# Attention with mask clusters: one row for the negated maximum, queries in token order, float64 words joined with two VectorE operations and one more on ScalarE

## The chip, the cores and the metric

The program runs on one core of one Trainium2 chip. The metric is the device time of one execution in microseconds (us), as the median of several runs. The core has five engines with a queue of instructions each: PE (TensorE, matmuls), DVE (VectorE), ACT (ScalarE), POOL (GpSimd) and SP (SyncE, which here issues DMAs).

## The reference, cut to what matters

Three layers follow each other: attention over 2 batches x 8 heads x 768 tokens x 64, in which a query sees only the keys of its own cluster; a dense layer 512 -> 2048 -> 512 with a Mish activation; and a layer of 8 experts with top-1 routing and a capacity.

```python
scale = 1.0 / np.sqrt(D)
q_assign = np.argmax(np.einsum('bhsd,hcd->bhsc', q_n, c_n), axis=-1)
k_assign = np.argmax(np.einsum('bhsd,hcd->bhsc', k_n, c_n), axis=-1)
mask = q_assign[:, :, :, None] == k_assign[:, :, None, :]
scores = scale * np.matmul(q, k.transpose(0, 1, 3, 2))
scores = np.where(mask, scores, -1000000000.0)
scores = scores - np.max(scores, axis=-1, keepdims=True)
attn = np.exp(scores)
attn = attn / (np.sum(attn, axis=-1, keepdims=True) + 1e-09)
...
h = x @ w_in
sp = np.where(h > 20.0, h, np.log1p(np.exp(np.minimum(h, 20.0))))
g = h * np.tanh(sp)
...
y = np.einsum('ecf,efd->ecd', np.maximum(np.einsum('ecd,edf->ecf', disp, w1), 0.0), w2)
```

The dense layer's weights arrive as float64, since a numpy scalar made them so; the kernel turns them into float32 itself.

## The kernel before

The order of every engine's instructions is the order in which the program is written (a manual schedule); nothing is moved later. Attention works on 8 pairs (one batch, two heads). `Attention.plan` (L472) gives each piece of work a step number, and `advance` (L616) runs the steps in order. A pair has 12 steps; step s scores one block of 128 keys against 384 queries of both heads (`score`, L374), runs `pv` (L405) for the step before, and computes one unit of row maxima for a pair further on (`max_unit`, L330: two matmuls on PE, one `reduce_max` on DVE, L346), 11 steps ahead. Two PSUM areas take turns for the scores and the maxima, so PE can begin the next unit of maxima only when DVE has read the last one. Where a function returns a closure, that runs at the head of the next step.

What the change touches:

- `load` (L202) reads queries, keys and values of a pair with the token number as `(p j)`: partition p holds the tokens 6p to 6p+5. The transposed columns are therefore in the order j, p and not in token order. `xparts` and `xnorm` (L454, L461) undo this where the attention's result is written: `norm3` (L464) writes the high part of x on ACT (L467) and its low part on DVE (L468) with every sixth column, 24 bytes apart.
- `max_split` (L348) runs on DVE at the end of each half pair (16 times): L353 writes the negated maximum rounded to fp32r, L354 copies it, L355 computes what the rounding left. `max_put` (L359) transposes these 12 columns on PE, copies them out of PSUM on ACT (L364), and sends them with four small DMAs into rows 96 and 97 of `QA`. `score` multiplies them with rows of ones in `KA`, which subtracts the maximum inside the matmul (98 rows).
- `Narrow` (L627) turns 32 chunks of float64 weights (128 x 512 words of 8 bytes) into float32, 28 of them inside the attention, 4 later (`rest`, L638). A chunk takes `bias` on ACT (L676: the high word times a power of two), then on DVE `up` (L680: shift left by 3), `low` (L685: the top three bits of the low word) and `sign` (L692), then a store. `plan` deals these out by `SLOTS`: 13 slots in 12 steps, three to a chunk, so that the order recurs every 36 steps.
- POOL adds up the exponentials (`add_up`, L394, L403) and applies the reciprocal sum (L442, L452).
- SP issues all loads, stores and the copies inside the chip (`spread`, L307).

```python
            for s, g in ((s0 - 1, N.bias), (s0, N.up), (s1, N.low), (s2, N.sign), (s2 + 1, N.store)):
                at(s, g, c)
```

Of the kernel before, what the change touches and what calls it, by code (L numbers as in the profile page):

```python
# [10 lines left out]
F32 = mybir.dt.float32  # L11
F32R = mybir.dt.float32r
BF16 = mybir.dt.bfloat16
I32 = mybir.dt.int32
U32 = mybir.dt.uint32
AF = mybir.ActivationFunctionType
ALU = mybir.AluOpType
AX = mybir.AxisListType
# [4 lines left out]
def f32(ap):  # L23
    return ap.bitcast(F32)
# [144 lines left out]
class Attention:  # L169
# [32 lines left out]
    def load(self, i, names):  # L202
        nc, S = self.nc, self.S
        b, hp = self.pairs[i]
        st = self.st.setdefault(i, {})
        for nm, src, bufs in (("q", self.q, 2), ("k", self.k, 1), ("v", self.v, 2)):
            if nm not in names:
                continue
            s = src[b, 2 * hp:2 * hp + 2].rearrange("h (p j) d -> p h j d", p=128)
            if nm == "v":  # L210
                t = self.p.tile([128, 2, self.NK, self.D], F32, tag=f"{nm}n", name=f"{nm}n{i}", bufs=bufs)
                nc.sync.dma_start(out=t, in_=s)
            else:
                t = self.early.tile([128, self.NK, 2, self.D], F32, tag=f"{nm}n", name=f"{nm}n{i}", bufs=bufs)
                for h in range(2):
                    nc.sync.dma_start(out=t[:, :, h, :], in_=s[:, h])
            st[nm] = t
# [129 lines left out]

    def max_split(self, i, r):  # L348
        nc, st = self.nc, self.st[i]
        m = st["m", r]  # L350
        mm = st["mm", r] = self.p.tile([128, 2, 2, 3], F32, tag="mm", name="mm")
        mr = self.p.tile([128, 2, 3], F32R, tag="mr", name="mr")
        nc.vector.tensor_scalar_mul(out=mr, in0=m, scalar1=-1.0)  # L353
        nc.vector.tensor_copy(out=mm[:, :, 0, :], in_=f32(mr))  # L354
        nc.vector.scalar_tensor_tensor(  # L355
            out=mm[:, :, 1, :], in0=m, scalar=-1.0, in1=f32(mr), op0=ALU.mult, op1=ALU.subtract
        )

    def max_put(self, i, r):  # L359
        nc, K, st = self.nc, self.K, self.st[i]  # L360
        pt = K.misc("pmt")
        nc.tensor.transpose(pt[0:12, 0:128], st["mm", r].rearrange("p h l t -> p (h l t)"), K.ident)
        mt = self.p.tile([12, 128], F32R, tag="mt", name="mt")
        nc.scalar.activation(out=mt, in_=pt[0:12, 0:128], func=AF.Copy)  # L364
        QA = self.QA[i % 3]
        for h in range(2):
            for l in range(2):
                e = nc.gpsimd if i + r + h == 0 else nc.sync
                e.dma_start(
                    out=f32(QA[96 + l:97 + l, h, 384 * r:384 * r + 384].rearrange("a (t p) -> a t p", t=3)),  # L370
                    in_=f32(mt[6 * h + 3 * l:6 * h + 3 * l + 3, :]),
                )

    def score(self, s):  # L374
        nc, K = self.nc, self.K
# [7 lines left out]
        for h in range(2):  # L383
            nc.tensor.matmul(  # L384
                ps[:, h, 0:384], lhsT=KB[:, h, ks], rhs=QB[:, h, qs], start=True, stop=False
            )
            nc.tensor.matmul(  # L387
                ps[:, h, 0:384], lhsT=KA[0:98, h, ks], rhs=QA[0:98, h, qs], start=False, stop=True
            )
        pt = self.p.tile([128, 2, 384], F32, tag="P", name="P", bufs=4)  # L390
        nc.scalar.activation(out=pt, in_=ps[:, :, 0:384], func=AF.Exp, scale=1.0 / float(self.D) ** 0.5)  # L391
# [62 lines left out]
    def xparts(self, i, r):  # L454
        b, hp = self.pairs[i]
        return (
            a[b][:, hp, :].rearrange("d (p j) -> d j p", j=6)[:, 3 * r:3 * r + 3, :]
            for a in (self.K.xh, self.K.xl)
        )

    def xnorm(self, i, r):  # L461
        return self.st[i]["x", r].rearrange("d (j p) -> d j p", j=3)

    def norm3(self, i, r):  # L464
        hi, lo = self.xparts(i, r)
        x = self.xnorm(i, r)
        self.nc.scalar.activation(out=hi, in_=x, func=AF.Copy, scale=-1.0)  # L467
        return lambda: self.nc.vector.scalar_tensor_tensor(  # L468
            out=lo, in0=x, scalar=-1.0, in1=f32(hi), op0=ALU.mult, op1=ALU.subtract
        )  # L470

    def plan(self, N):  # L472
# [50 lines left out]
        slots = [w for w in slots if w >= self.N0]  # L523
        for c in range(N.CUT):
            s0, s1, s2 = slots[3 * c:][:3]
            for s, g in ((s0 - 1, N.bias), (s0, N.up), (s1, N.low), (s2, N.sign), (s2 + 1, N.store)):
                at(s, g, c)
            if c + 3 < N.CUT:
                at(s2 + self.NL, N.load, c + 3)
# [97 lines left out]
class Narrow:  # L627
# [10 lines left out]
    def rest(self):  # L638
# [3 lines left out]
        for c in range(self.CUT, self.N):  # L642
            self.bias(c)
            yield
            self.up(c)
            yield
            self.low(c)
            yield
            self.sign(c)
            if c + 3 < self.N:  # L650
# [21 lines left out]
    def bias(self, c):  # L672
# [2 lines left out]
        r = self.res[c] = self.p.tile([128, 512], I32, tag="n32", name=f"n32_{c}", bufs=3 if c < self.CUT else 2)  # L675
        self.nc.scalar.activation(out=f32(r), in_=f32(hi), func=AF.Copy, scale=2.0 ** -112)  # L676

    def up(self, c):
        r = self.res[c]
        self.nc.vector.tensor_scalar(out=r, in0=r, scalar1=3, scalar2=None, op0=ALU.logical_shift_left)  # L680

    def low(self, c):
        lo, hi = self.words(c)
        r = self.res[c]
        self.nc.vector.scalar_tensor_tensor(  # L685
            out=r, in0=lo, scalar=29, in1=r, op0=ALU.logical_shift_right, op1=ALU.bitwise_or
        )

    def sign(self, c):
# [4 lines left out]
        )  # L694

    def run(self, c, store=True):
        for g in (self.bias, self.up, self.low, self.sign):
            g(c)

    def store(self, c):  # L700
# [989 lines left out]
```

## Time and profile before

| | us |
|---|---|
| median of 3 runs (840.01 to 846.32) | 843.99 |
| the profiled execution | 843.21 |
| its span on the core | 841.5 |
| busy: PE / DVE / ACT / POOL | 772.5 / 650.4 / 455.8 / 221.7 |

The attention takes the first 340 us or so of the span, the dense layer the time up to some 610 us, the experts the rest; the dense layer begins inside the attention's last steps. A row of the profile gives the busy time of an engine in a stretch, or a group of instructions with their mean time and with the idle time just before them and what ended it. The share of a whole span is a mean over stages with different limits, so the rows of one stage count.

### The profile page before, as it was taken

How to read it: one execution, taken by the hardware profiler on the slowest of the kernel's cores; microseconds unless marked ns; L12 is line 12 of the kernel's file. 1: busy time of each engine (PE TensorE's matmuls, PEld its weight loads, DVE VectorE, ACT ScalarE, POOL GpSimd, SP SyncE). 2: the span in 40 equal slices, each digit the busy share in tenths (PEclk: the TensorE clock that was granted, in tenths of full speed). 3: DMA queues.
4: the chain of work that ended last, by engine and by line, in shares of the span. 5: the costliest groups of instructions: out<-in, count | busy, mean ns of one | idle time of the engine just before them, and what ended most of it. 6: DMA issues, size and time to landing. Idle time of an engine off the chain costs nothing. (4 is left out here: it accounts for less than half of the span.)

```text
span 841.5 us, 12536 instructions
## 1 busy us (share of the span) xinstructions
PE 772.5 (92%) x4290; PEld 616.0 (73%) x4290; DVE 650.4 (77%) x1259; ACT 455.8 (54%) x867; POOL 221.7 (26%) x178
## 2 busy tenths in 40 slices
PE   7797898888888899898999999999999999999994
PEld 4564555555554456687898989999898999999994
DVE  5756899898999879999999758888857666566661
ACT  4144565656555567555555634444555655566552
POOL 4054565667667521000100003000031111101110
PEclk8898999999999899999999999999999999999998
DMA  7576768686766443877855635633244966787640
GB/s 173 115 199 176 204 169 205 177 226 184 190 170 156 131 128 125 302 279 265 305 184 194 211 110 189 190 135 116 75 125 137 315 217 216 241 276 244 190 140 21
DMA packets 118938, 155.83 MB, mean 185 GB/s; under 512 B 35154, under 2 KB 82450, under 8 KB 114772
## 3 DMA queue, kind: packets, MB, share of 16 engines
q1 hardware_dynamic: 114180, 131.88, 53.8%
q0 software_dynamic: 4688, 23.09, 6.9%
q8 instruction: 36, 0.59, 0.3%
q14 instruction: 34, 0.28, 0.1%
HBM read 93.65 MB, written 42.24 MB: 161 GB/s over the span
## 5 line engine op out<-in xcount | busy, mean ns | idle before, releaser
L391 ACT ACTIVATE P<-pst 128x768 f32<-128x768 f32 x96 | 77.8, 811 | 103.9 <-PE pst L387 99.4
L768 DVE TENSOR_TENSOR cut<-raw,cut 128x512 fp32r<-128x512 f32 x168 | 110.4, 688 | 26.3 <-ACT cut L767 15.5
L403 POOL TENSOR_TENSOR sum<-sum,P 128x768 f32<-128x768 f32 x52 | 104.1, 2002 | 6.9 <-ACT P L391 4.1
L767 ACT ACTIVATE cut<-raw 128x512 fp32r<-128x512 f32 x168 | 98.3, 623 | 2.7 <-DMA raw<-in_moe_w_dram 2.7
L1497 PE MATMUL y<-cut,hy 128*128 128x512 f32 x384 | 99.3, 394 | 0.0
L346 DVE TENSOR_REDUCE m<-pm 128x1 f32<-128x768 f32 x96 | 90.7, 949 | 8.8 <-PE pm L342 8.2
L1464 PE MATMUL he<-xeh,cut 128*128 128x256 f32 x512 | 92.4, 280 | 0.2 <-ACT xeh L1418 0.2
L342 PE MATMUL pm<-KA,QA 96*128 96x384 f32 x192 | 59.2, 392 | 31.8 <-DVE m L346 28.4
L1464 PEld LDWEIGHTS he<-xeh,cut 128*128 128x128 f32 x512 | 82.2, 188 | 5.5 <-ACT xeh L1418 0.4
L415 PE MATMUL acc<-P,vn 128*64 128x384 f32 x384 | 84.4, 519 | 0.5 <-ACT x L421 0.4
L835 ACT ACTIVATE r<-n,two 128x384 f32<-128x384 f32 x64 | 39.4, 616 | 83.7 <-DVE n L825 82.7
L1497 PEld LDWEIGHTS y<-cut,hy 128*128 128x128 f32 x384 | 67.6, 188 | 10.9
L384 PE MATMUL pst<-QB,KB 128*128 128x384 f32 x192 | 68.0, 354 | 6.8 <-DMA KB<-kl 5.9
L810 PE MATMUL ph<-xh,cut 128*128 128x384 f32 x256 | 67.0, 343 | 6.5 <-DVE t L847 3.7
L1464 PE MATMUL he<-xel,cut 128*128 128x256 f32 x256 | 71.5, 279 | 0.2 <-DVE xel L1419 0.2
L342 PEld LDWEIGHTS pm<-KA,QA 96*128 96x128 f32 x192 | 30.9, 200 | 51.5 <-DVE m L346 43.9
L810 PE MATMUL ph<-xh,again 128*128 128x384 f32 x256 | 66.7, 342 | 0.0
L387 PE MATMUL pst<-QA,KA 98*128 98x384 f32 x192 | 66.3, 345 | 0.0
L1509 POOL DMA_INDIRECT out_dram<-ye,meta x17 | 18.3, 1078 | 172.5 <-ACT ye L1507 141.8
L1469 ACT ACTIVATE hy<-he 128x256 fp32r<-128x256 f32 x64 | 24.5, 383 | 71.4 <-PE he L1464 71.4
L1470 DVE SCALAR_TENSOR_TENSOR hy<-he,hy 128x256 fp32r<-128x256 f32 x64 | 27.1, 424 | 44.3 <-ACT hy L1469 44.2
L871 PE MATMUL o<-cut,gh 128*128 128x512 f32 x192 | 59.8, 392 | 1.0 <-DVE rs L443 1.0
(231 smaller groups left out, 1717.3 us busy)
## 6 DMA issues: line engine op xcount, KB each, us to landing
raw<-in_moe_w_dram SPq DMA_DIRECT2D x72, 256.0 KB
raw<-in_moe_w_dram SPq DMA_DIRECT2D x36, 512.0 KB
kept<-cut POOLq DMA_DIRECT2D x16, 1024.0 KB, 8.4
again<-kept SPq DMA_DIRECT2D x16, 1024.0 KB
n<-in_moe_w_in_dram SPq DMA_DIRECT2D x16, 512.0 KB
n<-in_moe_w_out_dram SPq DMA_DIRECT2D x16, 512.0 KB
wf<-n SPq DMA_DIRECT2D x32, 256.0 KB
raw<-wf SPq DMA_DIRECT2D x16, 512.0 KB
```

The lines of the kernel that those rows point to most:

```text
L342: nc.tensor.matmul(ps[:, g, 0:384], lhsT=QA[0:96, h, q0:q0 + 128], rhs=KA[0:96, h, 384 * g:384 * g + 384], start=True, stop=True,)
L346: nc.vector.reduce_max(out=st["m", r][:, h, t:t + 1], in_=ps[:, :, 0:384], axis=AX.XY)
L384: nc.tensor.matmul(ps[:, h, 0:384], lhsT=KB[:, h, ks], rhs=QB[:, h, qs], start=True, stop=False)
L387: nc.tensor.matmul(ps[:, h, 0:384], lhsT=KA[0:98, h, ks], rhs=QA[0:98, h, qs], start=False, stop=True)
L391: nc.scalar.activation(out=pt, in_=ps[:, :, 0:384], func=AF.Exp, scale=1.0 / float(self.D) ** 0.5)
L403: e.tensor_add(out=st["sum", r], in0=st["P", w - 1] if t == 1 else st["sum", r], in1=st["P", w])
L415: nc.tensor.matmul(acc[64 * h:64 * h + 64, 0:384], lhsT=st["v"][:, h, t, :], rhs=pt[:, h, :], start=(t == 0), stop=(t == self.NK - 1),)
L767: nc.scalar.activation(out=t[:, 0, part], in_=raw[:, part], func=AF.Copy)
L768: self.low.tensor_sub(out=t[:, 1, part], in0=raw[:, part], in1=f32(t[:, 0, part]))
L810: nc.tensor.matmul(ps[:, 0:384], lhsT=w[:, k, :], rhs=x[:, k, sl], start=(k == 0 and j == 0), stop=(k == 3 and j == 2),)
L1464: nc.tensor.matmul(ps[:, 0:MAIN], lhsT=w[:, k, :], rhs=x[:, k, :], start=(k == 0 and j == 0), stop=(k == 3 and j == 2),)
L1497: nc.tensor.matmul(st["y"][s], lhsT=g[:, c], rhs=w, start=(f == 0 and j == 0), stop=(f == 7 and j == 2))
```

## The change

The queries are read as `(j p)`: partition p, slot j holds token 128j + p, so the columns come out in token order, and the result is written without a stride. Keys and values are read as before. The negated maximum has one row in place of two: the rounded value alone is transposed and sent (two DMAs in place of four a half pair), and the matmul has 97 rows. What the rounding leaves is a factor common to a row's exponentials and to their sum. `Narrow` has a new ACT operation `last` in place of the DVE operation `up`: it reads the top byte of the low word and writes floor(byte / 32), as an integer, over the low word; `up` is now the joined operation (shift left by 3, or with that integer).

```diff
@@ load
-            s = src[b, 2 * hp:2 * hp + 2].rearrange("h (p j) d -> p h j d", p=128)
+            order = "h (j p) d -> p h j d" if nm == "q" else "h (p j) d -> p h j d"
+            s = src[b, 2 * hp:2 * hp + 2].rearrange(order, p=128)
@@ max_split
-        mm = st["mm", r] = self.p.tile([128, 2, 2, 3], F32, tag="mm", name="mm")
-        mr = self.p.tile([128, 2, 3], F32R, tag="mr", name="mr")
-        nc.vector.tensor_scalar_mul(out=mr, in0=m, scalar1=-1.0)
-        nc.vector.tensor_copy(out=mm[:, :, 0, :], in_=f32(mr))
-        nc.vector.scalar_tensor_tensor(
-            out=mm[:, :, 1, :], in0=m, scalar=-1.0, in1=f32(mr), op0=ALU.mult, op1=ALU.subtract
-        )
+        mr = st["mr", r] = self.p.tile([128, 2, 3], F32R, tag="mr", name="mr")
+        nc.vector.tensor_scalar_mul(out=mr, in0=st["m", r], scalar1=-1.0)
@@ max_put
         for h in range(2):
-            for l in range(2):
-                e = nc.gpsimd if i + r + h == 0 else nc.sync
...
+            e = nc.gpsimd if i + r + h == 0 else nc.sync
+            e.dma_start(
+                out=f32(QA[96:97, h, 384 * r:384 * r + 384].rearrange("a (t p) -> a t p", t=3)),
+                in_=f32(mt[3 * h:3 * h + 3, :]),
+            )
@@ score
-                ps[:, h, 0:384], lhsT=KA[0:98, h, ks], rhs=QA[0:98, h, qs], start=False, stop=True
+                ps[:, h, 0:384], lhsT=KA[0:97, h, ks], rhs=QA[0:97, h, qs], start=False, stop=True
@@ xparts, norm3
-            a[b][:, hp, :].rearrange("d (p j) -> d j p", j=6)[:, 3 * r:3 * r + 3, :]
...
+            a[b][:, hp, 384 * r:384 * r + 384] for a in (self.K.xh, self.K.xl)
@@ plan
-            for s, g in ((s0 - 1, N.bias), (s0, N.up), (s1, N.low), (s2, N.sign), (s2 + 1, N.store)):
+            for s, g in ((s0 - 1, N.bias), (s1 - 1, N.last), (s1, N.up), (s2, N.sign), (s2 + 1, N.store)):
@@ Narrow
+    def last(self, c):
+        b = self.src[c].bitcast(U8).rearrange("p c (w b) -> p c w b", b=4)
+        lo, hi = self.words(c)
+        self.nc.scalar.activation(
+            out=lo, in_=b[:, :, 0, 3:4].rearrange("p c b -> p (c b)"), func=AF.Copy, scale=1 / 32, bias=-15.5 / 32
+        )
     def up(self, c):
-        r = self.res[c]
-        self.nc.vector.tensor_scalar(out=r, in0=r, scalar1=3, scalar2=None, op0=ALU.logical_shift_left)
-
-    def low(self, c):
         lo, hi = self.words(c)
         r = self.res[c]
         self.nc.vector.scalar_tensor_tensor(
-            out=r, in0=lo, scalar=29, in1=r, op0=ALU.logical_shift_right, op1=ALU.bitwise_or
+            out=r, in0=r, scalar=3, in1=lo, op0=ALU.logical_shift_left, op1=ALU.bitwise_or
         )
```

The instruction streams show what this does to the order. First, VectorE in steps 24 and 25, the two steps around the end of a half pair (L346 before and L348 after is `reduce_max`; L680 before is the old `up`, L685 is `low`; L680 after is the joined `up`; `kl` is a low part of split keys). Before:

```order
L346 TENSOR_REDUCE m<-pm 128x1
L353 TENSOR_SCALAR mr<-m 128x6
L354 COPY mm<-mr 128x2x3
L355 SCALAR_TENSOR_TENSOR mm<-m,mr 128x2x3
L680 TENSOR_SCALAR n_7_1215<-n_7_1215 128x512
L233 TENSOR_TENSOR kl_1245<-pt,kh_1244 128x384
L346 TENSOR_REDUCE m<-pm 128x1
L685 SCALAR_TENSOR_TENSOR n_7_1215<-n_7_1039,n_7_1215 128x512
```

After:

```order
L348 TENSOR_REDUCE m<-pm 128x1
L353 TENSOR_SCALAR mr<-m 128x6
L235 TENSOR_TENSOR kl_1217<-pt,kh_1216 128x384
L348 TENSOR_REDUCE m<-pm 128x1
L680 SCALAR_TENSOR_TENSOR n_7_1190<-n_7_1190,n_7_1019 128x512
```

Three instructions between the two reductions are gone; one stays beside the split.

Second, VectorE in steps 40 and 41 (L260 and L261, after L262 and L263, pick the cluster; L468, after L459, is the low part of x; `ks` are similarities). Before:

```order
L346 TENSOR_REDUCE m<-pm 128x1
L260 TENSOR_REDUCE mx<-qs_1688 128x12
L261 TENSOR_TENSOR e_1768<-qs_1688,mx 128x6x32
L680 TENSOR_SCALAR n_13_1739<-n_13_1739 128x512
L251 TENSOR_TENSOR ks_1758<-cl,psim 128x96
L346 TENSOR_REDUCE m<-pm 128x1
L685 SCALAR_TENSOR_TENSOR n_13_1739<-n_13_1542,n_13_1739 128x512
L468 SCALAR_TENSOR_TENSOR xl_75<-x,xh_73 128x3x128
```

After:

```order
L348 TENSOR_REDUCE m<-pm 128x1
L262 TENSOR_REDUCE mx<-qs_1649 128x12
L263 TENSOR_TENSOR e_1728<-qs_1649,mx 128x6x32
L253 TENSOR_TENSOR ks_1718<-cl,psim 128x96
L348 TENSOR_REDUCE m<-pm 128x1
L680 SCALAR_TENSOR_TENSOR n_13_1699<-n_13_1699,n_13_1507 128x512
L459 SCALAR_TENSOR_TENSOR xl_75<-x,xh_73 128x384
```

Four operations on two SBUF inputs, or in place, stood in these two steps, and now three; the last is contiguous.

Third, ScalarE in step 31, where the new operation meets the most work (L391, after L386, is the exponential; L364 and L274, after L360 and L276, copy the maxima and the one-hot rows; L676, after L667, is `bias`). Before:

```order
L391 ACTIVATE P<-pst 128x768
L364 ACTIVATE mt<-pmt 12x128
L274 ACTIVATE et<-pe 64x768
L676 ACTIVATE n_10_1491<-n_10_1325 128x512
L391 ACTIVATE P<-pst 128x768
```

After:

```order
L386 ACTIVATE P<-pst 128x768
L360 ACTIVATE mt<-pmt 6x128
L276 ACTIVATE et<-pe 64x768
L667 ACTIVATE n_10_1456<-n_10_1295 128x512
L673 ACTIVATE n_10_1295<-n_10_1295 128x512
L386 ACTIVATE P<-pst 128x768
```

One more operation (L673, `last`) stands between two exponentials.

## Rows read from the trace of the kernel before

**Rows 1.** The table of windows: three stretches of one pair's length inside the attention, and the beginning of the dense layer. After the bounds and the length: busy time of PE, PEld (weight loads), DVE, ACT and POOL, each with its count of instructions, then the granted clock as a share of 2.4 GHz, the share of the DMA engines, and GB/s.

```profile
118.00:156.00 38.00, 32.73 (x179) 20.25 (x178) 34.96 (x51) 22.61 (x39) 24.54 (x15) 1.00 0.76 199
156.00:194.00 38.00, 32.34 (x177) 19.99 (x177) 35.16 (x52) 22.41 (x38) 24.44 (x15) 1.00 0.74 184
...
345.00:430.00 85.00, 80.24 (x397) 70.45 (x396) 79.66 (x169) 48.89 (x99) 7.18 (x22) 1.00 0.82 288
```

**Rows 2.** The waits between 118 and 268 us, where each pair still has all its work: who waited for whom, us in total, times, longest.

```profile
PE pm L342 <- DVE m L346: 19.8, 16, 2.5
```

**Rows 3.** Single lines of the whole span: count, then the shortest, median and longest duration in ns, then the first and last start in us.

```profile
L355 DVE SCALAR_TENSOR_TENSOR mm<-m,mr x16: 156/160/1808, 31.4 to 304.5; 128x6 f32<-128x6 f32 x16
...
L680 DVE TENSOR_SCALAR n<-n x32: 406/418/2050, 52.5 to 389.5; 128x512 int32<-128x512 int32 x32
...
L468 DVE SCALAR_TENSOR_TENSOR xl<-x,xh x16: 859/1572/2460, 72.1 to 340.5; 128x384 fp32r<-128x384 f32 x16
```

**Rows 4.** The timeline of POOL between 110 and 176 us: start, duration of the whole run of instructions, how many.

```profile
111.98 8.45 POOL L403 TENSOR_TENSOR sum<-sum,P 128x768 f32<-128x768 f32 x4
...
129.51 7.92 POOL L403 TENSOR_TENSOR sum<-sum,P 128x768 f32<-128x768 f32 x4
...
167.28 7.92 POOL L403 TENSOR_TENSOR sum<-sum,P 128x768 f32<-128x768 f32 x4
```

**Rows 5.** The timeline of DVE in step 24, at the end of a half pair: start and duration in us.

```profile
117.20 0.94 DVE L346 TENSOR_REDUCE m<-pm 128x1 f32<-128x768 f32 x1
118.18 0.36 DVE L353 TENSOR_SCALAR mr<-m 128x6 fp32r<-128x6 f32 x1
...
118.65 1.80 DVE L355 SCALAR_TENSOR_TENSOR mm<-m,mr 128x6 f32<-128x6 f32 x1
120.37 0.41 DVE L680 TENSOR_SCALAR n<-n 128x512 int32<-128x512 int32 x1
...
121.18 0.94 DVE L346 TENSOR_REDUCE m<-pm 128x1 f32<-128x768 f32 x1
```

**Rows 6.** The timeline of DVE in steps 36 to 38, again around the end of a half pair.

```profile
156.14 1.81 DVE L355 SCALAR_TENSOR_TENSOR mm<-m,mr 128x6 f32<-128x6 f32 x1
157.87 0.68 DVE L685 SCALAR_TENSOR_TENSOR n<-n,n 128x512 int32<-128x512 int32 x1
...
158.94 0.94 DVE L346 TENSOR_REDUCE m<-pm 128x1 f32<-128x768 f32 x1
...
161.16 0.94 DVE L346 TENSOR_REDUCE m<-pm 128x1 f32<-128x768 f32 x1
```

**Rows 7.** The timeline of DVE in steps 40 and 41.

```profile
166.87 0.95 DVE L346 TENSOR_REDUCE m<-pm 128x1 f32<-128x768 f32 x1
...
169.25 2.05 DVE L680 TENSOR_SCALAR n<-n 128x512 int32<-128x512 int32 x1
...
171.38 0.95 DVE L346 TENSOR_REDUCE m<-pm 128x1 f32<-128x768 f32 x1
...
173.46 2.46 DVE L468 SCALAR_TENSOR_TENSOR xl<-x,xh 128x384 fp32r<-128x384 f32 x1
...
176.00 0.95 DVE L346 TENSOR_REDUCE m<-pm 128x1 f32<-128x768 f32 x1
```

**Rows 8.** The timeline of PE in steps 39 and 40: the starts of two units of maxima, one step apart, in steps that also compute similarities.

```profile
163.44 0.52 PE L342 MATMUL pm<-KA,QA 96*128 96x384 f32 x2
...
166.22 0.51 PE L342 MATMUL pm<-KA,QA 96*128 96x384 f32 x2
```

**Rows 9.** The timeline of DVE in step 29.

```profile
133.88 0.95 DVE L346 TENSOR_REDUCE m<-pm 128x1 f32<-128x768 f32 x1
134.75 1.00 DVE L680 TENSOR_SCALAR n<-n 128x512 int32<-128x512 int32 x1
...
138.21 0.95 DVE L346 TENSOR_REDUCE m<-pm 128x1 f32<-128x768 f32 x1
```

**Rows 10.** Groups of instructions by line and shape over the whole span: count, then busy us in all and mean ns of one, then the idle time before them.

```profile
L391 ACT ACTIVATE P<-pst 128x768 f32<-128x768 f32 x96 | 77.8, 811 | 103.9 <-PE pst L387 99.4 <-POOL x L442 2.2 <-POOL x L452 1.3
...
L854 DVE SCALAR_TENSOR_TENSOR gl<-t,gh 128x384 fp32r<-128x384 f32 x64 | 35.3, 552 | 0.6 <-ACT gh L844 0.6
...
L844 ACT ACTIVATE gh<-t 128x384 fp32r<-128x384 f32 x64 | 32.6, 509 | 3.8 <-DVE t L841 3.8
...
L676 ACT ACTIVATE n<-n 128x512 f32<-128x512 f32 x32 | 21.2, 661 | 0.0
...
L467 ACT ACTIVATE xh<-x 128x384 fp32r<-128x384 f32 x16 | 14.8, 927 | 2.6 <-DVE x L447 2.6
...
L274 ACT ACTIVATE et<-pe 64x768 bf16<-64x768 bf16 x8 | 6.4, 802 | 3.7 <-PE pe L270 3.7
...
L364 ACT ACTIVATE mt<-pmt 12x128 fp32r<-12x128 f32 x16 | 4.3, 267 | 7.1 <-PE pmt L362 6.2
```

**Rows 11.** The same groups between 345 and 430 us alone, where the last four chunks are joined.

```profile
L680 DVE TENSOR_SCALAR n<-n 128x512 int32<-128x512 int32 x4 | 1.7, 423 | 0.0
```

**Rows 12.** DMA packets between 3 and 6 us, while the first queries and keys are read.

```profile
DMA packets 2691, 0.68 MB, mean 225 GB/s; under 512 B 2691, under 2 KB 2691, under 8 KB 2691
```

**Rows 13.** The waits between 60 and 340 us: the longest one of PE for a DMA (at 72 us, at the head of the second pair).

```profile
PE pst L384 <- DMA KB<-kl: 5.9, 1, 5.9
```

More of the change, by code (lines that the diff above doesn't have):

```diff
@@ L15 @@
 U32 = mybir.dt.uint32
+U8 = mybir.dt.uint8
 AF = mybir.ActivationFunctionType
@@ L349, in max_split @@
         nc, st = self.nc, self.st[i]
-        m = st["m", r]
-        mm = st["mm", r] = self.p.tile([128, 2, 2, 3], F32, tag="mm", name="mm")
-        mr = self.p.tile([128, 2, 3], F32R, tag="mr", name="mr")
-        nc.vector.tensor_scalar_mul(out=mr, in0=m, scalar1=-1.0)
-        nc.vector.tensor_copy(out=mm[:, :, 0, :], in_=f32(mr))
-        nc.vector.scalar_tensor_tensor(
-            out=mm[:, :, 1, :], in0=m, scalar=-1.0, in1=f32(mr), op0=ALU.mult, op1=ALU.subtract
-        )
+        mr = st["mr", r] = self.p.tile([128, 2, 3], F32R, tag="mr", name="mr")
+        nc.vector.tensor_scalar_mul(out=mr, in0=st["m", r], scalar1=-1.0)
     def max_put(self, i, r):
@@ L361, in max_put @@
         pt = K.misc("pmt")
-        nc.tensor.transpose(pt[0:12, 0:128], st["mm", r].rearrange("p h l t -> p (h l t)"), K.ident)
-        mt = self.p.tile([12, 128], F32R, tag="mt", name="mt")
-        nc.scalar.activation(out=mt, in_=pt[0:12, 0:128], func=AF.Copy)
+        nc.tensor.transpose(pt[0:6, 0:128], f32(st["mr", r]).rearrange("p h t -> p (h t)"), K.ident)
+        mt = self.p.tile([6, 128], F32R, tag="mt", name="mt")
+        nc.scalar.activation(out=mt, in_=pt[0:6, 0:128], func=AF.Copy)
         QA = self.QA[i % 3]
         for h in range(2):
-            for l in range(2):
-                e = nc.gpsimd if i + r + h == 0 else nc.sync
[L369 to L372, printed above, removed]
+            e = nc.gpsimd if i + r + h == 0 else nc.sync
[3 more added lines that the diff above has]
+            )
     def score(self, s):
@@ L456, in xparts @@
         return (
-            a[b][:, hp, :].rearrange("d (p j) -> d j p", j=6)[:, 3 * r:3 * r + 3, :]
-            for a in (self.K.xh, self.K.xl)
-        )
-    def xnorm(self, i, r):
-        return self.st[i]["x", r].rearrange("d (j p) -> d j p", j=3)
+            a[b][:, hp, 384 * r:384 * r + 384] for a in (self.K.xh, self.K.xl)
+        )
     def norm3(self, i, r):
         hi, lo = self.xparts(i, r)
-        x = self.xnorm(i, r)
+        x = self.st[i]["x", r]
         self.nc.scalar.activation(out=hi, in_=x, func=AF.Copy, scale=-1.0)
@@ L644, in rest @@
             yield
+            self.last(c)
+            yield
             self.up(c)
-            yield
-            self.low(c)
             yield
@@ L696, in run @@
     def run(self, c, store=True):
-        for g in (self.bias, self.up, self.low, self.sign):
+        for g in (self.bias, self.last, self.up, self.sign):
             g(c)
```

## The prediction

> **What bounds the kernel now.** I read the table of windows first, for where the change has room to act. In one pair's time inside the attention (38.0 us) PE is busy 32.3 to 32.7 us, DVE 35.0 to 35.2 us, ACT 22.4 to 22.6 us [rows 1]. DVE is fullest and PE still has some 5.5 us of idle time in each pair. The list of waits says what ends that time: between 118 and 268 us PE stands idle 19.8 us, 16 times, until DVE has read the row maxima (L346) [rows 2]. So in this stage a microsecond on DVE is worth something, but only in those steps in which DVE comes last.
>
> The timelines tell which steps these are, and why. A step that also computes similarities takes PE 2.78 us when nothing holds it (163.44 to 166.22) [rows 8]; one with a split takes 2.22 us (158.94 to 161.16) [rows 6]. Steps 40 and 41 took 4.51 and 4.62 us [rows 7], step 29 4.33 us [rows 9], step 24 3.98 us [rows 5]. In each, DVE instructions last far longer than they need: L680 2.05 us where its shortest is 0.41 us, L468 2.46 us where its shortest is 0.86 us, L355 1.80 us where its shortest is 0.16 us [rows 3, 5, 7]. The POOL timeline explains it: four additions of about 2.0 us stand there back to back, from 111.98 to 120.43 and from 167.28 to 175.20 us [rows 4]. L355 ends at 120.45, L680 at 171.30: each has waited for the addition in progress to end. The reduction (L346, from PSUM) takes 0.94 or 0.95 us all the same. So such an instruction costs its own time plus what is left of POOL's addition, and two of them in a row, with a reduction between, cost one addition each.
>
> **The rule that speaks against this change.** The Trainium skill has this as a rule ("SBUF — State Buffer", section "Who interferes with whom"): a DVE instruction with two SBUF inputs, or in a mode that uses both ports, and a GpSimd instruction that reads SBUF hold a shared port in turn, and the second one blocks until the first ends. The rows above agree: 1.80 us for an instruction of 0.16 us. By it a wait does not vanish with the instruction that suffered it; the next such instruction inherits it. That is my first rival, priced below from rows.
>
> **The change, part by part.** I cost each part by the steps in which DVE is late. Elsewhere PE is last, and DVE time costs nothing; the cover there is PE's own 2.22 to 2.78 us a step.
>
> *The old `up` (L680) goes.* Step 40 then holds the reduction, the pick and an addition from PSUM, about 2.75 us on DVE, so PE's 2.78 us set it: 1.73 us less than 4.51. In step 41 the joined `up` and the low part of x still wait, but the latter gets its turn one POOL addition (1.98 us) sooner and is itself 0.31 us shorter (below): 2.3 us less by the end of both steps. In step 29 L680 took the turn that L468 wanted; without it the step falls from 4.33 to PE's 2.78, 1.55 us less. The slots recur after 36 steps, so step 65 gives the same 1.55. Sum 5.4 us. The joined `up` costs what `low` cost (same shape, one strided input): 0.68 us where POOL is quiet [rows 6].
>
> *The copy and the remainder of the maximum (L354, L355) go.* In step 24 (and 60) nothing is left that waits for POOL after L353: 3.98 us falls to PE's 2.22, 1.76 us each, 3.5 us. In steps 36, 48, 72 and 78 an `up` or `sign` follows directly, as L685 does at 157.87 [rows 6]: it inherits the wait, and only the two instructions' own time, 0.17 + 0.16 us, is saved: 1.3 us. The transpose has 6 columns in place of 12 and the matmul 97 rows in place of 98: nothing, since neither sets the number of columns that stream.
>
> *The low part of x is contiguous.* The shortest strided L468 is 0.86 us [rows 3]; the same operation without a stride, L854, takes 0.55 us [rows 10]: 0.31 us less. It stands in late steps; six are not counted above (17, 35, 47, 53, 71, 77): 1.8 us. On ACT the high part falls from 0.93 to about 0.51 us (L467 against L844) [rows 10], which helps pay for the next part.
>
> *`last` on ACT.* No row shows it. Its nearest is `bias` (L676), the same shape read 8 bytes apart: 0.66 us [rows 10]. If writing 8 bytes apart cost what writing 24 apart costs L467 (0.42 us for 384 elements, so 0.56 for 512), it would be 1.22 us. I take 0.66, since 8 bytes is L676's stride. Per pair that is 4.33 x 0.66 = 2.9 us more, 0.8 less by the high parts: ACT goes from 22.5 to about 24.6 us of a pair, far from full. It costs where several operations meet: step 31 has the exponential, L364, L274, `bias` and now `last`, 0.81 + 0.27 + 0.80 + 0.66 + 0.66 = 3.2 us [rows 10], about 0.4 to 1 us more than PE needs there; it recurs at step 67, and a handful of steps come to 2.8 or 2.9 us. I take +1.4 us in all; the bounds are 0 (hidden by ACT's idle time) and 28 x 0.66 = 18.5 us (all on the path). Queued behind `last` is the next exponential, for which PE's `pv` waits; the joined `up` waits for `last`, which is issued a step earlier.
>
> *The queries' order.* While the first queries and keys are read, all 2691 packets are under 512 B, 253 B on average [rows 12]: the destination interleaves two heads, so the pieces are already 64 floats. The new order changes addresses, not packets: nothing. If they were read half as fast, the start would move by the time of the first 0.39 MB at 225 GB/s, 1.7 us; later pairs are loaded eight steps ahead of use.
>
> *Half of the small DMAs go.* SP issues 31 in place of 62. PE waited once for a DMA, 5.9 us at 72 us [rows 13], behind large transfers and not behind these: nothing; at most 1.3 us (two issues) if SP's queue were what was late. That wait stays.
>
> *The dense layer.* Four `up` operations of 0.42 us, 1.7 us [rows 11], in a stretch where DVE has 79.7 of 85 us and PE 80.2 [rows 1]: both nearly full, so I count half, 0.8 us. The later stages are left alone.
>
> **The sum.** 5.4 + 3.5 + 1.3 + 1.8 = 12.0 us in the attention, 0.8 in the dense layer, less 1.4 for ACT: 11.4 us. From the profiled execution's 843.2 us that is 831.8, say 832. The median of the runs shown, 843.99, is 0.8 us above that execution, too little to correct for.
>
> **The rivals.**
>
> *The waits are passed on.* Each turn that an instruction gives up is taken by another, and the steps keep their POOL additions. Then only own times count: 0.31 us in some twelve steps with a low part of x (3.7), 0.33 in six with the maximum (2.0), 0.8 in the dense layer, less 1.4: 5.1 us, 838. For it: rows 6, where the next instruction stands ready. Against it: in steps 24 and 40 no such instruction is left.
>
> *PE becomes the bound throughout.* With three waiters in place of four, the others fall between POOL's additions more often, and PE's idle time for the maxima goes: 19.8 us in 150 us [rows 2], about 30 over the 228 us from the second pair to the last maxima. All of it would give 812; with 1 us or two lost to ACT and part of it kept, 818. Against it: four additions back to back leave no gap to fall into.
>
> *Slower: `up` waits for `last`.* `last` stands behind the exponential and other copies in ACT's queue; if `up` reaches DVE's head before it is done, DVE stands, with the next reduction queued behind it and PE waiting for that. If that wait were 0.9 us in each of 28 chunks (an exponential late), it costs 25 us and the time is 857. It decides from 11.4 / 28 = 0.41 us a chunk. For it: 3.2 us of ACT work in step 31. Against it: `last` is issued one step earlier, and ACT is idle about 40% of a pair [rows 1].
>
> **How the numbers follow.** Chances: the forecast (824 to 835.5) 0.50, waits passed on 0.28, PE the bound 0.13, slower 0.09. About 1%, or 8.4 us, is what a measurement here can tell from no change. Faster by more than that holds the forecast and PE the bound, a little cut at the edge: 0.62; within 1% 0.29; slower 0.09. The range of 820 to 842 leaves out half of "PE the bound", all of "slower", and a few hundredths of "passed on": 0.2. The forecast's own range is 824 to 835.5.
>
> **What would show it.** DVE should be busy some 4 to 5 us less in a pair, PE's wait for L348 between the same steps should fall from 19.8 to about 12 us, and steps 24, 29 and 40 should take PE's 2.2 to 2.8 us. `last` should read 0.66 us, the low part of x 0.55 at its shortest, and the first transposes should start where they did. I am wrong if step 24 or 40 still lasts over 4 us (waits passed on), if DVE shows idle time before `up` ended by ACT (the slower rival), or if PE has almost no idle time before the maxima (PE the bound).

## The result, and the profile after

The changed kernel takes 811.51 us (median of 4 runs, 809.26 to 812.88), the kernel before 845.15 us on the same chip: a ratio of 0.9609 [0.9559, 0.9659], 33.6 us less. The direction was forecast, the size was not: 832 us was said, with a range down to 820. The profiled execution has a span of 807.4 us against 841.5 (34.1 us less).

The page and the windows of one pair's time (107.2 to 140.2 us is step 24 to step 36) answer to [rows 1].

```profile
PE 764.9 (95%) x4289; PEld 611.2 (76%) x4290; DVE 617.2 (76%) x1195; ACT 468.1 (58%) x899; POOL 218.4 (27%) x177
```

```profile
107.20:140.20 33.00, 32.16 (x180) 19.99 (x178) 28.61 (x41) 24.05 (x43) 23.34 (x15) 1.00 0.86 231
140.20:172.90 32.70, 31.22 (x174) 19.54 (x170) 29.51 (x42) 22.96 (x41) 24.14 (x15) 1.00 0.89 219
```

A pair takes 33 us in place of 38, and PE is busy for all but 0.8 to 1.5 us of it. DVE now has time to spare: 28.6 to 29.5 us of work in such a pair, against some 35 us before.

The waits of PE in steps 25 to 72 (109 to 242 us), which answer to [rows 2]:

```profile
PE pm L344 <- DVE m L348: 5.8, 6, 2.2
```

16 waits of 19.8 us became 6 of 5.8 us, where some 12 us was said. Single lines of the whole span, shortest / median / longest ns, answer to [rows 3] and to the durations that the prediction took from [rows 10]:

```profile
L673 ACT ACTIVATE n<-n x32: 641/672/712, 49.2 to 355.4; 128x512 int32<-128x512 uint8 x32
```

```profile
L680 DVE SCALAR_TENSOR_TENSOR n<-n,n x32: 676/684/2369, 50.4 to 356.1; 128x512 int32<-128x512 int32 x32
```

```profile
L459 DVE SCALAR_TENSOR_TENSOR xl<-x,xh x16: 537/948/2171, 68.0 to 306.3; 128x384 fp32r<-128x384 f32 x16
```

`last` takes 0.67 us (0.66 was taken), the joined `up` 0.68, the low part of x 0.54 at its shortest (0.55). The prices were right; what they stood in the way of was not.

Where the time went, by the starts of the reductions (L346 before, L348 after) in the two traces: 1.9 us up to step 0, 8.3 us in steps 0 to 12, 22.9 us in steps 13 to 83, and 1.1 us in all that follows. Within steps 13 to 83, us in all (the differences are taken before rounding):

| steps | before | after | less | forecast |
|---|---|---|---|---|
| 24, 36, 48, 60, 72, 78 (end of a half pair) | 24.9 | 14.5 | 10.4 | 4.8 |
| 29, 65 | 8.7 | 4.2 | 4.4 | 3.1 |
| 40, 41 | 9.1 | 6.9 | 2.2 | 2.3 |
| 35, 47, 71, 77 | 15.5 | 11.5 | 3.9 | 1.2 |
| 16, 17, 28, 52, 53, 64 | 28.4 | 27.8 | 0.5 | 0.6 |
| 79 to 83 | 14.7 | 11.0 | 3.6 | 0 |
| 19, 55 | 4.1 | 8.2 | -4.1 | 0 |
| all others | 114.0 | 112.1 | 1.9 | -1.4 |

Step 24 took 2.53 us ([rows 5] before), step 29 2.10 [rows 9], steps 40 and 41 2.83 and 4.07 [rows 7]. The timeline of DVE in the last two: the pick and the addition from PSUM leave step 40 to PE, and in step 41 the joined `up` and the low part of x still wait, 1.00 and 2.17 us.

```profile
150.57 0.95 DVE L348 TENSOR_REDUCE m<-pm 128x1 f32<-128x768 f32 x1
...
153.41 0.95 DVE L348 TENSOR_REDUCE m<-pm 128x1 f32<-128x768 f32 x1
154.27 1.00 DVE L680 SCALAR_TENSOR_TENSOR n<-n,n 128x512 int32<-128x512 int32 x1
155.22 2.17 DVE L459 SCALAR_TENSOR_TENSOR xl<-x,xh 128x384 fp32r<-128x384 f32 x1
...
157.47 0.94 DVE L348 TENSOR_REDUCE m<-pm 128x1 f32<-128x768 f32 x1
```

### The profile page after: what moved, and what is told of

It reads as the page before. It is cut to its first block, busy times and chain, and to the rows that moved or that the text cites. A ratio compares the mean times of both kernels' runs of the same rounds, so it can differ in the third digit from the quotient of the medians.

```text
span 807.4 us, 12395 instructions
## 1 busy us (share of the span) xinstructions
PE 764.9 (95%) x4289; PEld 611.2 (76%) x4290; DVE 617.2 (76%) x1195; ACT 468.1 (58%) x899; POOL 218.4 (27%) x177
## 4 chain that ended last, share of the span: by engine, by line
PE 68%; DVE 18%; issue 5%; ACT 4%; DMA 3%; SPq 1%; POOL 0%; POOLq 0%; DVEq 0%; ACTq 0%
PE ph L805 12%; PE o L866 11%; PE he L1459 9%; PE y L1492 9%; PE acc L410 5%; PE pm L344 4%; PE pst L379 3%; DVE m L348 3%; PE pst L382 3%; PE psim L246 2%; DVE xl L459 2%; DVE cut L763 1%; DVE n L687 1%; DVE n L820 1%; DVE n L680 1%
## 5 line engine op out<-in xcount | busy, mean ns | idle before, releaser
L386 ACT ACTIVATE P<-pst 128x768 f32<-128x768 f32 x96 | 77.8, 810 | 63.9 <-PE pst L382 59.6
L348 DVE TENSOR_REDUCE m<-pm 128x1 f32<-128x768 f32 x96 | 90.7, 949 | 10.5 <-PE pm L344 10.2
L1492 PEld LDWEIGHTS y<-cut,hy 128*128 128x128 f32 x384 | 67.6, 188 | 10.9
L344 PE MATMUL pm<-KA,QA 96*128 96x384 f32 x192 | 57.0, 379 | 14.4 <-DVE m L348 12.1
L382 PE MATMUL pst<-QA,KA 97*128 97x384 f32 x192 | 65.3, 340 | 0.0
L866 PE MATMUL o<-again,gh 128*128 128x512 f32 x192 | 60.3, 395 | 0.0
```

The costliest lines, as they stand in the source:

```text
L344: nc.tensor.matmul(ps[:, g, 0:384], lhsT=QA[0:96, h, q0:q0 + 128], rhs=KA[0:96, h, 384 * g:384 * g + 384], start=True, stop=True,)
L348: nc.vector.reduce_max(out=st["m", r][:, h, t:t + 1], in_=ps[:, :, 0:384], axis=AX.XY)
L382: nc.tensor.matmul(ps[:, h, 0:384], lhsT=KA[0:97, h, ks], rhs=QA[0:97, h, qs], start=False, stop=True)
L866: nc.tensor.matmul(self.acc[t], lhsT=g[:, c], rhs=w, start=(f == 0 and j == 0), stop=(f == self.NF - 1 and j == 2),)
L1492: nc.tensor.matmul(st["y"][s], lhsT=g[:, c], rhs=w, start=(f == 0 and j == 0), stop=(f == 7 and j == 2))
```

## What the half pair's end shows

Here the forecast said that `up` or `sign` would inherit the wait of the remainder (L355). The timelines of DVE and POOL in step 36, first before (the two rows that [rows 6] lack, and the addition):

```profile
155.69 0.34 DVE L353 TENSOR_SCALAR mr<-m 128x6 fp32r<-128x6 f32 x1
156.06 0.17 DVE L354 COPY mm<-mr 128x6 f32<-128x6 f32 x1
```

```profile
156.07 1.84 POOL L403 TENSOR_TENSOR sum<-sum,P 128x768 f32<-128x768 f32 x1
```

And after, DVE and the two additions on POOL:

```profile
140.25 0.94 DVE L348 TENSOR_REDUCE m<-pm 128x1 f32<-128x768 f32 x1
141.22 0.34 DVE L353 TENSOR_SCALAR mr<-m 128x6 fp32r<-128x6 f32 x1
141.48 0.68 DVE L680 SCALAR_TENSOR_TENSOR n<-n,n 128x512 int32<-128x512 int32 x1
...
142.55 0.94 DVE L348 TENSOR_REDUCE m<-pm 128x1 f32<-128x768 f32 x1
```

```profile
139.52 2.02 POOL L398 TENSOR_TENSOR sum<-sum,P 128x768 f32<-128x768 f32 x1
```

```profile
141.61 2.23 POOL L398 TENSOR_TENSOR sum<-sum,P 128x768 f32<-128x768 f32 x1
```

The negation (L353) ends at 141.56, 0.02 us after an addition (139.52 + 2.02 = 141.54). It has one SBUF input and yet has waited for that addition itself: it takes 0.16 to 0.17 us where none runs beside it, and in all ten steps of the changed kernel in which one does, it lasts 0.34 to 1.71 us and ends some 0.03 us after it. What stands right behind it on DVE, `up`, starts at 141.48, before POOL's next addition at 141.61: it runs its 0.68 us without a wait, and POOL's addition is the one that gets longer (2.23 us, where that of before took 1.84). Before, the copy came next; the remainder behind it could start at 156.14 only, after the addition at 156.07, and waited for all of it. So between two additions of POOL there is a gap of less than 0.1 us (141.54 to 141.61) in which DVE can take the turn, and one instruction was too late for it by 0.07 us. That became theory A; the rival was that only own lengths count.

## The experiments

**The parts alone, on the kernel before.** One row for the maximum:

```diff
-        pt[0:12, 0:128], st["mm", r] ... KA[0:98, h, ks] ... four DMAs
+        pt[0:6, 0:128], f32(st["mr", r]) ... KA[0:97, h, ks] ... two DMAs
```

> The kernel before with the one row for the maximum alone (L354 and L355 gone, 31 small DMA issues on SP in place of 62). Turns: a DVE instruction that must wait for POOL's addition is gone from the end of each half pair, and the steps there (4 us) shorten by up to 1.7 us each; with some ten such steps 8 to 12 us off, if the next instruction comes too late or too early to inherit the wait. Passed on: `up`, `low` or `sign` follow and wait in its place, 0.33 us in six steps, 2 us off. Either way it is open whether the 5.9 us wait of PE for the keys' low part at 72 us goes (6 us more off) since two pairs of small DMAs ahead of it are gone.

828.86 us, 0.9785 [0.9716, 0.9854]. The six ends of half pairs fall from 24.9 to 13.5 us: this part, forecast at 4.8 us, brings some 17 us in all. In its trace 9.6 of them lie in steps 13 to 83 and 2.4 in step 12.

The order of the queries:

```diff
-            s = src[b, 2 * hp:2 * hp + 2].rearrange("h (p j) d -> p h j d", p=128)
+            order = "h (j p) d -> p h j d" if nm == "q" else "h (p j) d -> p h j d"
```

> The kernel before with the queries' order alone (x written without a stride). Own lengths: 0.31 us in some twelve late steps, 4 us off. Turns: the shorter instruction also lets the next one fall in front of a POOL addition in a few steps, 6 to 8 us off. If the reads of queries in the new order were slow, the start would come 1 to 2 us later and the first step after the start would show it.

840.89 us, 0.9931 [0.9894, 0.9968]: some 5 us, between the two values that were said.

The joined words:

```diff
-            for s, g in ((s0 - 1, N.bias), (s0, N.up), (s1, N.low), (s2, N.sign), (s2 + 1, N.store)):
+            for s, g in ((s0 - 1, N.bias), (s1 - 1, N.last), (s1, N.up), (s2, N.sign), (s2 + 1, N.store)):
```

> The kernel before with the joined words alone. Turns: steps 29, 40, 41 and 65 lose one waiter, 5.4 us off, 0.8 in the dense layer, less up to 1.4 for `last` on ACT: 5 us off; with `up` gone behind L355 as well, step 24 and 60 lose only 0.4 us each. ACT as the bound: `up` waits for `last` and the time stays or rises.

836.07 us, 0.9864 [0.9796, 0.9932]: some 10 us, where 5 were said. Steps 29 and 65 fall from 8.7 to 4.9 us, 40 and 41 from 9.1 to 7.2.

**The wait for the keys, on the kernel before.** `BS` is the distance in steps between the four kinds of copies; with 1 in place of 2 the low parts of the keys, the last of the four, are sent three steps earlier:

```diff
-    N0, N1, BS, NL = 4, 0, 2, 0
+    N0, N1, BS, NL = 4, 0, 1, 0
```

> The kernel before with the copies of low queries and of keys to the second operand (the four kinds of spread that follow each other at two steps' distance) at one step's distance, so that the keys' low part is sent three steps earlier. If PE's 5.9 us wait at 72 us is worth its length and the slow clock behind it (half speed from 78 to 85 us, some 2.5 us), 7 to 9 us off. If the DMA engines are the limit there, the wait stays or moves to another transfer: within 2 us of before.

843.64 us, 0.9966 [0.9921, 1.0011]. Step 12 falls from 9.2 to 3.9 us, but by step 54 the kernel is 1.3 us later than before (215.4 against 214.1). Of what came back, 5.3 us lie in steps 13, 14, 19, 43 and 44, where the granted clock is 0.50 to 0.96 (0.90 to 1.00 in the kernel before). At the port, what steps 32, 34 and 46 lose, 35 and 47 gain.

**One idle instruction put back into the changed kernel.** The remainder, without the copy, read by nobody:

```diff
+        nc.vector.scalar_tensor_tensor(
+            out=ml, in0=st["m", r], scalar=-1.0, in1=f32(mr), op0=ALU.mult, op1=ALU.subtract
+        )
```

> The changed kernel (811.5 us) with one idle operation put back behind the negated maximum: the remainder of 2 x 3 elements as before, two SBUF inputs, some 0.16 us, written to a tile that nobody reads. Nothing else of the second row is there: one row, six columns, half of the small DMAs. Theory A (a turn behind POOL's addition was what the second row cost): it waits again for an addition in progress in the six late steps 24, 36, 48, 60, 72 and 78, where some 1.8 us each came free, so about 11 us slower than the changed kernel, 818 to 826 us, and those steps last 4.0 to 4.3 us in place of 2.1 to 2.6. Rival B (only the work itself counted: own lengths, the copy, the DMAs): 0.16 us in 14 places, at most 2.3 us, 811 to 814 us, and the steps stay at 2.1 to 2.6 us.

821.25 us, 0.9749 [0.9665, 0.9832]. 9.7 us more than the changed kernel, for 16 instructions of 0.17 us. Steps 36, 48, 72 and 78 are back at 4.1 to 4.2 us (7.1 us in all), but 24 and 60 stay at 2.5: theory A erred there, as no other two-input instruction follows in them. The timeline of DVE in step 36, and the addition on POOL:

```profile
146.61 0.34 DVE L353 TENSOR_SCALAR mr<-m 128x6 fp32r<-128x6 f32 x1
146.99 0.17 DVE L355 SCALAR_TENSOR_TENSOR ml<-m,mr 128x6 f32<-128x6 f32 x1
147.10 2.31 DVE L684 SCALAR_TENSOR_TENSOR n<-n,n 128x512 int32<-128x512 int32 x1
```

```profile
147.01 1.85 POOL L402 TENSOR_TENSOR sum<-sum,P 128x768 f32<-128x768 f32 x1
```

The remainder starts 0.02 us ahead of the addition and takes the turn; `up` (L684) comes 0.09 us after the addition has started and waits for it.

A reduction in the same place, one SBUF input:

```diff
+        nc.vector.reduce_max(out=ml, in_=self.st[i]["m", r], axis=AX.X)
```

> The same place in the changed kernel, but the idle operation is a reduction of the 2 x 3 maxima to 2 x 1: one SBUF input, also short, nobody reads it. Theory A: it asks for no turn, so it costs its own length where DVE is last (six steps by some 0.1 to 0.2 us, about 1 us) and the time is 811 to 814 us. Rival B: the same time as with the remainder, within 1.5 us. If this one is as slow as the remainder, a turn at the port is not what makes the difference.

815.28 us (811.39 to 819.41), 0.9655 [0.9553, 0.9757]; the interval doesn't separate it from the changed kernel or from the remainder. The trace does: steps 13 to 83 take 196.9 us (196.4 in the changed kernel, 203.9 with the remainder).

**The same idle copy, of two operands.** Of the negated maxima, and of the maxima:

```diff
+        nc.vector.tensor_copy(out=ml, in_=f32(mr))
```

> The changed kernel with an idle copy of the 2 x 3 negated maxima behind the negation (0.17 us, one SBUF input, nobody reads the result). Theory A': POOL's additions and VectorE's instructions with two SBUF inputs take turns, and the turn goes to what stands right behind the instruction that the end of an addition released. In steps 36, 48, 72 and 78 the negation ends within 0.03 us of an addition and `up` or `sign` starts 0.05 to 0.13 us ahead of the next one, so it has no wait. The copy of mr can't start before the negation has ended, so `up` comes after the next addition has started and waits for all of it: four steps of 4.0 to 4.3 us in place of 2.3 to 2.6, some 7 us, 817 to 821 us. Rival (own lengths): 0.17 us where VectorE is last, at most 2 us, 811.5 to 814 us.

```diff
+        nc.vector.tensor_copy(out=ml, in_=st["m", r])
```

> The same copy, but of the maxima ahead of the negation: it doesn't wait for the negation's result, so it can start while that ends (the idle reduction did so 0.09 us ahead of the negation's end, and `up` behind it still came 0.07 us before the addition). Theory A': `up` keeps its turn, no wait in steps 36, 48, 72 and 78, 811 to 815 us, at least 4 us less than with the copy of mr. Rival (own lengths): the same time as with the copy of mr, within 2 us. If the copy holds the port itself, both lose the turn and theory A' says nothing of it.

823.13 us, 0.9727 [0.9639, 0.9815], against 813.54 us, 0.9594 [0.9529, 0.9660]: 9.6 us between two kernels with the same instructions of the same length. Steps 13 to 83 take 206.5 and 195.7 us. Of these 10.7 us, 6.9 lie in steps 36, 48, 72 and 78 (4.1 to 4.2 us each against 2.4 to 2.5), as theory A' had it; 4.5 lie in steps 38, 74, 75 and 80, where the granted clock is 0.58 to 0.88 with the copy of mr and 1.00 with that of m. Step 36 with the copy of mr, DVE and POOL:

```profile
147.45 0.34 DVE L353 TENSOR_SCALAR mr<-m 128x6 fp32r<-128x6 f32 x1
147.82 0.17 DVE L355 COPY ml<-mr 128x6 f32<-128x6 f32 x1
147.93 2.30 DVE L682 SCALAR_TENSOR_TENSOR n<-n,n 128x512 int32<-128x512 int32 x1
```

```profile
147.84 1.84 POOL L400 TENSOR_TENSOR sum<-sum,P 128x768 f32<-128x768 f32 x1
```

And with the copy of m:

```profile
142.72 0.34 DVE L353 TENSOR_SCALAR mr<-m 128x6 fp32r<-128x6 f32 x1
142.98 0.16 DVE L355 COPY ml<-m 128x6 f32<-128x6 f32 x1
143.05 0.68 DVE L682 SCALAR_TENSOR_TENSOR n<-n,n 128x512 int32<-128x512 int32 x1
```

```profile
143.11 2.30 POOL L400 TENSOR_TENSOR sum<-sum,P 128x768 f32<-128x768 f32 x1
```

A copy that needs the negation's result starts 0.03 us after it ends, and `up` comes 0.09 us after the addition has started. A copy that doesn't need it starts 0.08 us before the negation ends, and `up` is 0.06 us ahead of the addition. Theory A holds, with the place of each turn; own lengths can't tell these kernels apart. Whether the copy of mr, 0.02 us ahead of the addition, takes the turn itself or only makes `up` late isn't shown.

The Trainium skill ("SBUF — State Buffer", section "Who interferes with whom") says that of two such instructions the one that issues first has the ports for its whole length. These rows agree, and add how little decides it: 0.06 us one way, 0.09 us the other.

**Four small DMAs again, on the changed kernel.** Each head's row in two pieces:

```diff
-            e.dma_start(out=f32(QA[96:97, h, 384 * r:384 * r + 384] ...
+            for u, v in ((0, 2), (2, 3)):
+                e.dma_start(out=f32(QA[96:97, h, 384 * r + 128 * u:384 * r + 128 * v] ...
```

> The changed kernel with the row of the maximum written by four small DMAs in place of two (each head's row cut in two and one token tiles), 62 issues on SP's queue as before. Theory S (the four small DMAs held up the queue, so the low parts of the keys for the second pair came late and PE waited): step 12, 3.6 us in the changed kernel and 9.2 before, is over 6 us again, and the time 814 to 818 us. Rival (the wait went for another reason): step 12 stays under 5 us and the time is 811 to 813 us.

816.30 us (810.66 to 817.47), 0.9618 [0.9546, 0.9689]. The medians lie 4.8 us apart, but the runs overlap. The waits of PE between 60 and 90 us, and after them the longest wait of PE that the changed kernel has there (timeline of PE):

```profile
PE pst L380 <- DMA KB<-kl: 4.3, 1, 4.3
```

```profile
69.50 0.42 PE L379 MATMUL pst<-QB,KB 128*128 128x384 f32 x1 [0.75 <-issue]
```

The wait of [rows 13] is back, and step 12 lasts 8.9 us (3.7 in the changed kernel). In every kernel here with two small DMAs this step takes 3.7 to 6.8 us; in every one with four it takes 8.9 to 9.3, but for the one with the earlier keys.

**The changed kernel with the other parts undone.** Two rows again, the old joining again, the old order again, one line of each edit:

```diff
-        mr = st["mr", r] = self.p.tile([128, 2, 3], F32R, tag="mr", name="mr")
+        mm = st["mm", r] = self.p.tile([128, 2, 2, 3], F32, tag="mm", name="mm")
```

> The changed kernel with the two rows of the maximum put back (copy, remainder, 12 columns, four small DMAs in place of two, 98 rows), the rest as changed. The one row alone took 17 us off the kernel before. If the parts add up (theory A: each removes waits of its own), it is 825 to 831 us. If the parts share waits (rival: with the joined words in place, the remainder finds the port free more often), it is 815 to 822 us. Steps 24, 36, 48, 60, 72 and 78 then tell: about 4.2 us each by theory A, under 3 us by the rival.

```diff
-        for g in (self.bias, self.last, self.up, self.sign):
+        for g in (self.bias, self.up, self.low, self.sign):
```

> The changed kernel with the old joining of the float64 words (three VectorE operations, the third with two SBUF inputs and another that shifts in place) and no work of it on ScalarE. Joining alone took 10 us off the kernel before. If the parts add up: 820 to 824 us, with steps 29, 40 and 41 and their recurrences 36 steps on at 4.3 to 4.6 us. If they share waits: 813 to 817 us.

```diff
-            a[b][:, hp, 384 * r:384 * r + 384] for a in (self.K.xh, self.K.xl)
+            a[b][:, hp, :].rearrange("d (p j) -> d j p", j=6)[:, 3 * r:3 * r + 3, :]
```

> The changed kernel with the queries read in the old order, so that x is written and its two parts are read 24 bytes apart again. The order alone took 6 us off the kernel before (0.9931 [0.9894, 0.9968]), of which its profile shows 1.8 us between steps 13 and 84. The three parts alone give 17.9 us there, together they give 22.9. If the missing 5 us belong to the order (the shorter low part of x only pays once the other waits are gone), steps 13 to 84 last some 5 to 7 us longer than in the changed kernel, and it takes 817 to 820 us. If parts add up, 1.5 to 2.5 us more there and 813 to 815 us.

828.50 us, 0.9813 [0.9729, 0.9898]; 819.83 us, 0.9726 [0.9632, 0.9821]; 821.98 us, 0.9770 [0.9679, 0.9861]. The two rows cost 17 us both ways, the joining 8 to 10; steps 13 to 83 take 13.8, 7.1 and 5.0 us more than in the changed kernel (9.6, 6.5 and 1.8 less when each is put in alone). So the order of the queries is worth 5 us there once the other waits are gone, and 1.8 while they stand; the sum of the parts alone (17.9 us) falls short of the whole (22.9) because the order's and the maximum's parts bring more when the others are there. These are single traces, and the 1.8 us are the least sure: with the order alone, steps 19, 55 and 74 take 1.5 us more each at a granted clock of 0.53 to 0.63, and steps 79 to 83 take 3.6 us less. The beginning of the dense layer, from its first matmul to the 65th, is longer in the kernels with the old order (before, one row alone, joining alone, this one: 33.8 or 33.9) and 32.4 or 32.5 in those with the new: 1.3 us also belong to the order. The last three high and low parts of x stand in this stretch; one wait of PE for DVE falls from 1.7 to 1.0 us there, and two of 0.4 us go.

**Two versions that might be faster.** The changed kernel with `BS` at 1 (the keys' low parts are computed when they were and sent three steps earlier, not one), and with the joining moved out of steps 4 and 5 of a pair:

```diff
-    N0, N1, BS, NL = 4, 0, 2, 0
+    N0, N1, BS, NL = 4, 0, 1, 0
```

> The changed kernel with the low parts of the keys computed and sent one step earlier (the planner's BS 2 to 1). In the kernel before this took 5 us off step 12 and all of it was given back by step 54. Here step 12 has some 1 us of waiting left. If the order of the other operations is as good: 808 to 811 us; if the moved operations meet POOL's additions: 811 to 816 us. I expect no measurable difference, 811 us.

```diff
-    SLOTS = (1, 1, 2, 1, 1, 1, 1, 1, 2, 1, 1, 0)
+    SLOTS = (1, 1, 2, 1, 0, 0, 1, 2, 2, 2, 1, 0)
```

> The changed kernel with the joining of the words taken out of steps 4 and 5 of each pair, where four of POOL's additions stand back to back and both `up` and the pick wait (steps 16, 17, 28, 52, 53 and 64 last 4.3 to 4.8 us each, 27.8 us in all), and put into steps 7 and 9. If the turns at the port are the cause, `up` and `sign` run without a wait at their new places: each of the six steps falls by up to one addition less what the pick still waits, some 1.3 us each, 7 to 8 us in all, and 803 to 806 us. If another waiter takes each turn, 810 to 813 us. If steps 7 and 9 are then the late ones (two joins of 0.68 us each on top of the rest), 813 to 818 us.

811.55 us, 0.9568 [0.9501, 0.9635], and 812.59 us, 0.9629 [0.9524, 0.9734]: neither can be told from the changed kernel, and the 803 to 806 us of the second were missed. The moved joining takes 9.0 us off the six steps at POOL's additions (27.8 to 18.8), as turns at the port say, but 3.3 us come back in steps 29 and 65 and some 5 us in other steps, where the low part of x or a moved join now has the wait, and steps 0 to 12 are 5.4 us longer, 2.7 of them in steps 0 to 2 (see below on these). What is left of the six steps' waits can be moved; PE, busy 32.2 of 33 us, has little left to give.

## Why the prediction was wrong

*"The waits are passed on" and "inherits the wait" (steps 36, 48, 72, 78; 0.33 us each).* This is the step that failed most. Each gave 1.7 to 1.9 us, 7.5 in all where 1.3 were said. The rule behind it, that a wait goes to the next two-input instruction, left out that the instruction right behind one which an addition's end has released starts ahead of the next addition (141.48 against 141.61 above). [rows 6] showed it already: L685 ran its 0.68 us straight behind L355, without a wait. The ends of half pairs give 10.4 us where 4.8 were said; 24 and 60, said at 3.5, gave 2.9.

*"That wait stays" (KB<-kl; small DMAs nothing, at most 1.3 us).* This step failed too, and the reading behind it: PE waits for a DMA a second time, 1.3 us for `QB<-ql` between 118 and 268 us. Two issues less do bring some 1.3 us: from the first small DMA to the first of the keys' low parts SP takes 6.95 us in place of 8.29. But the wait of 5.9 us behind it went to 0.8, and with it the fall of the clock: granted 0.58 between 78 and 85 us before, 1.00 in the same steps after. Step 12 gave 5.5 us. Putting the four DMAs back brought it back, so the count of small DMAs is shown as its cause; why the time from issue to use is also some 2.5 us longer with them (8.1 us against 5.6) stays open. The other 2.7 us of steps 0 to 12 aren't the change's. All but 0.1 of them lie in steps 0 to 2, which take 11.1 us before and 8.5 after; the changed kernel with `BS` at 1, whose instructions are the same up to there, takes 10.9 in them, at a granted clock of 0.69 in place of 1.00.

*The clock was in no term.* In steps 79 to 83 nothing was said to change, and 3.6 us went. These are the windows of the two kernels there, before and then after:

```profile
288.00:296.00 8.00, 7.16 (x22) 4.49 (x24) 5.38 (x8) 1.92 (x3) 0.99 (x1) 0.57 0.36 113
```

```profile
258.50:269.50 11.00, 10.93 (x55) 6.30 (x55) 10.19 (x14) 6.94 (x11) 4.02 (x3) 1.00 0.44 144
```

Before, PE had stood idle 1.42, 0.63 and 1.20 us between 283 and 289, and then the granted clock was near 1.2 GHz; after, only one wait of 1.07 us is left there and the clock stays at 2.4. It goes the other way in steps 19 and 55: after a wait of 2.2 us for the maxima each lasts 4.1 us where it lasted 2.0, at a clock of 0.52 (below). Before, a wait of 2.5 us stands in the same place and the clock stays at 1.00 behind it. Nor is it settled for steps 79 to 83 that the shorter waits kept the clock up: in the kernel before with the queries' order alone, PE stood idle 1.13, 0.61 and 1.20 us in the same places, the clock stayed at 1.00, and the five steps took 11.0 us. The waits alone don't decide: in the changed kernel with two rows, after waits of 2.2 us both times, step 19 took 2.4 us at a clock of 1.00 and step 55 took 3.9 us at 0.56. So the runs show what a lower clock costs, but not that this change removed its cause.

```profile
92.00:95.50 3.50, 3.50 (x16) 1.49 (x14) 1.60 (x3) 1.08 (x2) 1.54 (x1) 0.52 1.05 220
```

*The joining (5.4 us)* was sized well where it was worked out, 2.2 of 2.3 us in steps 40 and 41, and too low in 29 and 65, which fall to 2.10 us and not to the 2.78 that was taken: 4.4 in place of 3.1.

*The low part of x (0.31 us in six steps)* has its own time right, but where it holds the port it also lengthens the addition behind it (2.32 and 2.34 us at steps 35 and 47 before, 2.02 and 2.03 after); steps 35, 47, 71 and 77 gave 3.9 us, step 47 alone 1.75 of them, with the joining's help.

*ScalarE (1.4 us lost)*: a pair has 23.0 to 24.1 us of ACT's work, 24.6 was said. `up` waited for `last` once, 0.3 us; the slower rival didn't occur. The 1.4 us can't be found among the steps.

*The dense layer (0.8 us)*: 1.3 us, but from the queries' order, which was said to change nothing there. The joined `up` there takes 0.69 us, four times, where the old pair took 0.42 and 0.68.

The rival "PE becomes the bound" came nearest: 818 us, or 812 with all of PE's idle time gone (30 us off 843.2 is 813). Its condition, more gaps to fall into with three waiters in place of four, was doubted because four additions back to back leave none. They leave one of less than 0.1 us each, and that was enough. That the time met its 812 us is in part luck: 14.0 of the 19.8 us of waits went, not all, and 5.5 us of step 12 and 4.4 us ahead of step 3, the latter not the change's, came on top. The 1.9 us before step 0 are not explained by the change: over the changed kernel and those made from it step 0 starts at 35.0 to 40.8 us.

## What to carry to other kernels

Before saying that a wait is inherited, look at what stands right behind the instruction that the wait ends with: it may take the turn, and an instruction between the two that needs the first one's result can lose it, whatever its own length. Where PE waits, price a lower clock after the wait as well, from a stretch of the same trace in which it fell, and as a range: after the same wait of 2.2 us a step here took 2.4 or 3.9 us. And count the issues ahead of a late transfer on its queue, however small they are.

## What the runs showed of the hardware that was not expected

Two kernels with the same instructions, which differ in which operand a copy of 0.17 us reads, are 9.6 us apart; 6.9 us of it stand in the four steps in which `up` or `sign` loses its turn. Four small DMAs in place of two, 3 KB in all both times, put 16.0 us in place of 12.5 between the first of them and the use of the 192 KB transfers issued behind them on SP's queue: 3.5 us, of which the two issues themselves are 1.0. The same program's start varies: the granted clock between 16 and 24 us was 0.50 in the kernel with the idle remainder and 1.00 in the changed kernel, whose instructions are the same up to then, and runs of one kernel lie up to 12 us apart (841.16 to 853.37 us for the kernel before on one chip).
